# Attention, gated MLP and SoLU MLP on one core: low parts of the early weights on VectorE, low bits of twelve blocks on ScalarE, the first block's products by piece into one bank, means from split sums, and a new order

## The chip, the core and the metric

The kernel runs on one core of a Trainium2 chip. Its engines are TensorE (PE, the matmuls), VectorE (DVE), ScalarE (ACT), GpSimd (POOL) and SyncE (SP, which issues nearly all transfers). Each engine plays its own instructions in order, and semaphores hold it where an operand is missing. The metric is the time of one execution on the device in microseconds; the median of the runs shown counts.

## The reference

```python
def reference(**kwargs):
    attn_out = _attn_ref(**attn_kwargs)          # q, k, v: 4 x 8 x 576 x 64; window 32, for half the heads dilated by 4
    x = attn_out.transpose(0, 2, 1, 3).reshape(B * S, H * D)      # 2304 x 512
    x = _moe_ref(x=x, **moe_kwargs)
    return _moe2_ref(x=x, **moe2_kwargs)

def _moe_ref(x, w_gate, w_val, w_out, rms_g):    # 512 -> 1536 -> 512
    rms = np.sqrt(np.mean(x * x, axis=-1, keepdims=True) + 1e-06)
    xn = x / rms * rms_g
    g = xn @ w_gate
    silu = g * (1.0 / (1.0 + np.exp(-g)))
    return silu * (xn @ w_val) @ w_out

def _moe2_ref(x, w_in, w_out, g_ln):             # 512 -> 1024 -> 512
    h = x @ w_in
    solu = h * softmax(h)
    return layer_norm(solu) * g_ln @ w_out
```

The weights come in 64-bit words, and each is taken apart into a high and a low float32r part.

## The kernel before

Nine pieces of 256 tokens (`PIECES`, t = 0 to 8) form five parts (`PARTS`); the first part is the pieces 0 and 1. For each piece attention makes x, `rms` norms it and splits it into `xh` and `xl`, and `mlp` multiplies it with twelve blocks f of the 1536 hidden columns, each block with a gate product `g`, a value product `vp`, tanh, silu and product on ACT and DVE, and an out product into the banks y0 to y3. Every product is three in float32r, high by high, low by high and high by low (`mm3`, L952 to L954). `g` and `vp` have one PSUM bank each.

Weights: a block of 512 KB is fetched by SP (`fetch`, `raw`), shifted on ACT (`shifted`, L386), its low bits are taken on DVE (`parts`, L391), both are joined on DVE (`joined`, L395), ACT casts the high part (`halves`, L333) and DVE or POOL subtracts it for the low part (`lows`, L342). A block f has three such weights, 0 `w_gate`, 1 `w_val`, 2 `w_out`. A raw block lies where its weights will be, in slot f.

Pieces 0 and 1 are done first, as four pairs of head groups (`pair(t, m)`). Their q, k and v lie in the rooms of slots 11 to 8 (`EARLY`: pair (0,0) in 11, (0,1) in 10, (1,0) in 9, (1,1) in 8), so the weights of these slots can be fetched only when a pair's values are done. A pair runs scores (L509, L511), maximum, a centring product (L522), exponential, sum, weights, transposes (L544) and values (`pv`, L566). The later pieces go through `attention`. `rms` takes the mean of squares, for t of 2 and more as one float32 product of ones with the sum (`ms`, L827).

`mlp` runs over virtual passes: v = 0 is piece 0 with f = 0 alone, v = 1 piece 1 with f = 0 alone, both 256 columns wide, and v = 2 both pieces with the other blocks, 512 wide.

The order is made by `Plan`: each step has its needs, its buffers, a cost for each engine it may use and a due time; a greedy pass over the engines gives the order, and `play` writes the program in it. `NUDGE` shifts due times of single steps and `ENGINE` fixes engines. Where the plan has a hole on TensorE early on, `fill` (L351) issues products of a constant `seed` (128x256, bf16) into a bank that the next step takes.

Of the kernel before, what the change touches and what calls it, by code (L numbers as in the profile page):

```python
# [20 lines left out]
P = 128  # L21
# [23 lines left out]
def groups_of(piece):  # L45
# [30 lines left out]
    else:  # L76
# [7 lines left out]
        for at, bt in ((128, b), (192, b2)):  # L84
# [12 lines left out]
HALVES = 1  # L97
# [5 lines left out]
SINGLE = 7  # L103
# [6 lines left out]
NUDGE = {('centred', (1, 1)): -15.5, ('copy', (1, 0)): 10, ('copy', (3, 1)): 11, ('copy', (4, 1)): 57,  # L110
         ('copy', (5, 0)): 32, ('copy', (7, 1)): 50, ('ecomb', 5): -17, ('eload', 9): 14, ('eps', 1): -41.9,
         ('eps', 3): 13, ('ewhole', 1, 0): -45, ('ewhole', 2, 1): 35, ('ewhole', 3, 0): 48, ('ewhole', 4, 0): 15,
         ('exps', (2, 1)): 57, ('g', 2, 8, 1): 24, ('gln',): 60, ('high', 0, 0): -27, ('high', 1, 0): 35,
         ('landed', 6): -22, ('load_qk', (1, 1)): -1.6, ('load_v', (0, 0)): 3.07, ('low', 0, 1): -43.6,
         ('low', 1, 0): 93, ('low', 1, 1): -32.8, ('masking', (2, 0)): -65, ('masking', (3, 1)): -22,
         ('masking', (4, 1)): 40, ('masking', (5, 0)): 13, ('masking', (6, 0)): -65, ('maximum', (1, 0)): -3,
         ('maximum', (1, 1)): -8.1, ('maximum', (2, 0)): -98, ('maximum', (3, 1)): -45, ('maximum', (5, 1)): 78,
         ('newton', 0, 2): 58, ('norm', (0, 1)): -0.8, ('norm', (2, 1)): 31, ('out', 2, 1, 0): -124,
         ('out', 2, 1, 1): 45.1, ('out', 2, 2, 0): 7.5, ('prod', 1, 0): 28, ('prod', 3, 0): 43, ('prod', 4, 3): 23,
         ('prod', 4, 7): 71, ('rmsg',): 14, ('scale', 0, 1): -35.9, ('scale', 1, 0): -11.5, ('scale', 1, 1): -38.4,  # L120
         ('scale', 1, 2): 0.08, ('scale', 1, 4): 1, ('scale', 2, 0): -5.5, ('scale', 2, 1): -25, ('scale', 2, 3): 49,
         ('scale', 3, 0): -11.4, ('scale', 3, 1): -38.8, ('scale', 3, 4): 43, ('silu', 3, 3): 17, ('silu', 3, 4): 46,
         ('square', 0, 0): 77, ('square', 0, 1): -34.9, ('square', 1, 1): -32.9, ('square', 1, 4): -10,
         ('square', 2, 1): -42.3, ('square', 3, 1): -29.9, ('sums', (1, 0)): -45, ('sums', (1, 1)): 44,
         ('tanh', 'c11', 0): 138, ('total', 2, 0): -12, ('total', 3, 0): -9.1, ('turned0', (0, 1)): -34,
         ('turned1', (0, 1)): -38, ('uhigh', 3, 4): -68, ('ulow', 4, 2): 88, ('ulow', 4, 4): 1, ('xcomb', 't3'): 35,
         ('xcomb', 't4'): 44, ('xlow', 't1', 1): 8, ((1, 0), 'lows', 0): 19, ((1, 0), 'lows', 1): 11,
         ((1, 0), 'shifted', 2): 33, ((1, 1), 'fetch', 0): 41, ((1, 1), 'fetch', 1): 12, ((1, 1), 'fetch', 2): 6,
         ((1, 1), 'joined', 0): 5.2, ((1, 1), 'joined', 2): -10, ((1, 1), 'lows', 2): -16.5,
         ((1, 1), 'parts', 1): 10, ((1, 1), 'parts', 2): 47.5, ((1, 1), 'shifted', 1): 91,  # L130
         ((1, 1), 'shifted', 2): 41, ((1, 10), 'fetch', 2): -33, ((1, 10), 'parts', 0): 23,
         ((1, 11), 'fetch', 0): -52, ((1, 11), 'fetch', 1): 31.9, ((1, 11), 'fetch', 2): -32,
         ((1, 11), 'lows', 0): 19.5, ((1, 11), 'parts', 0): 22.9, ((1, 2), 'fetch', 1): -5,
         ((1, 2), 'joined', 1): 32, ((1, 2), 'lows', 1): 91, ((1, 2), 'parts', 0): 4.7, ((1, 2), 'parts', 1): -4,
         ((1, 2), 'parts', 2): 39, ((1, 3), 'fetch', 1): 32, ((1, 3), 'halves', 2): 8.4, ((1, 3), 'joined', 2): 18.2,
         ((1, 3), 'parts', 0): 28, ((1, 3), 'parts', 1): 11.7, ((1, 3), 'parts', 2): 35, ((1, 3), 'shifted', 0): 13,
         ((1, 4), 'fetch', 0): 45, ((1, 4), 'fetch', 1): 27, ((1, 4), 'fetch', 2): 35.82, ((1, 4), 'halves', 2): -41,
         ((1, 4), 'joined', 0): 15.8, ((1, 4), 'joined', 2): 18, ((1, 4), 'lows', 1): -4.6, ((1, 4), 'lows', 2): -20,
         ((1, 4), 'parts', 1): 3.3, ((1, 4), 'parts', 2): -25, ((1, 5), 'fetch', 0): 16, ((1, 5), 'fetch', 1): 33,
         ((1, 5), 'lows', 2): 36.9, ((1, 5), 'parts', 0): 24.1, ((1, 5), 'parts', 1): 33.9,  # L140
         ((1, 5), 'parts', 2): 11.7, ((1, 6), 'fetch', 0): -3.5, ((1, 6), 'fetch', 1): 29,
         ((1, 6), 'halves', 0): -12, ((1, 6), 'joined', 0): 28, ((1, 6), 'lows', 1): 42, ((1, 6), 'parts', 0): 24.5,
         ((1, 6), 'parts', 2): 28, ((1, 7), 'fetch', 0): 74, ((1, 7), 'fetch', 2): -54, ((1, 7), 'joined', 0): 21.7,
         ((1, 7), 'parts', 0): -29.1, ((1, 8), 'fetch', 0): -21, ((1, 8), 'fetch', 1): 82.9,
         ((1, 8), 'parts', 0): 17.8, ((1, 9), 'fetch', 1): 18.2, ((1, 9), 'parts', 0): 19}
# [43 lines left out]
class Plan:  # L189
# [20 lines left out]
    def order(self):  # L210
# [32 lines left out]
        while ready:  # L243
# [13 lines left out]
            if e == "p" and free["d"] > start:  # L257
                free["d"] += 0.45 * cost
# [27 lines left out]
def tile_attention_glu_solu(ctx: ExitStack, tc: tile.TileContext, qk_d, v_d, w1_d, win2_d, wout2_d,  # L286
# [71 lines left out]
    def prepare(stage, f, cuts, srcs, scales, dues, needs=(), lead=((1, 0), "joined", 0)):  # L358
# [65 lines left out]
        for i in range(m):  # L424
            plan.add((key, "fetch", i), {"s": 1.35}, fetch(i), needs, due=dues[i] - 12)
        for n, c in enumerate(cuts):
            w, due = 512 * len(c), dues[c[0]]
            one, two, act, pool_ = 0.15 + w / 1920, 0.15 + w / 960, 0.2 + w / 1200, 0.25 + w / 500
            plan.add((key, "shifted", n), {"a": act}, shifted(c), [(key, "fetch", i) for i in c], due=due)
            plan.add((key, "parts", n), {"d": one}, parts(c), [(key, "fetch", i) for i in c], due=due)  # L430
# [32 lines left out]
    def pair(t, m, due):  # L463
# [61 lines left out]
        def exps(e):  # L525
            nc.scalar.activation(T[s_], T[sp], AF.Exp, scale=0.125)
# [53 lines left out]
        plan.add(step("load_qk"), {"s": 2.15}, load_qk, due=due - 8)  # L580
# [1376 lines left out]
```

## Time and profile before

| what | us |
|---|---|
| runs | 711.44, 711.47, 712.87 (median 711.47) |
| the profiled execution | 712.27, span 710.2 |
| TensorE busy | 702.3 (99%), 4533 matmuls |
| DVE busy | 509.4 (72%) |
| ACT busy | 358.9 (51%) |
| POOL busy | 135.5 (19%) |
| last product's end | 707.05 |

The page gives each engine's busy time over the whole span; where TensorE waits is read from its timeline, in which a line shows in brackets how long the engine stood idle before an instruction and what ended that. An instruction's own duration runs past the start of the next on TensorE, so the time that a product takes is read from one start to the next.

### The profile page before, as it was taken

The numbers are of one execution on the slowest core, as the hardware profiler recorded it, in microseconds if no ns is written. First come the engines' busy times: TensorE is split into PE (matmuls) and PEld (weight loads), VectorE is DVE, ScalarE is ACT, GpSimd is POOL, SyncE is SP. The second block draws the span as 40 slices with busy tenths as digits, with TensorE's granted clock in tenths as the row PEclk, the third lists the DMA queues.
The fourth block names the chain that finished last, engine by engine and source line by source line (L and its number), as shares of the span: only waits on it lengthen the run. The fifth ranks groups of instructions, "written<-read, shape, count | busy, mean of one in ns | idle before, by whom it ended". The sixth has DMA issues, their size and how long they took to land.

```text
span 710.2 us, 11738 instructions
## 1 busy us (share of the span) xinstructions
PE 702.3 (99%) x4533; PEld 593.3 (84%) x4533; DVE 509.4 (72%) x932; ACT 358.9 (51%) x769; POOL 135.5 (19%) x166
## 2 busy tenths in 40 slices
PE   8999999999999999999999999999999999999998
PEld 6788888899998888888888888888888888888887
DVE  5899899679585986668966766689677677665552
ACT  2976854344535554516655554355375555543440
POOL 0322432250506121110000000014044311010110
PEclk9999999999999999999999999999999999999999
DMA  9999433154368764403321112947032111000001
GB/s 336 401 407 354 133 101 118 64 185 141 134 225 293 276 206 141 141 7 125 123 72 37 52 60 97 344 139 220 1 119 75 60 60 45 30 16 30 30 30 45
DMA packets 42424, 97.21 MB, mean 137 GB/s; under 512 B 3841, under 2 KB 14081, under 8 KB 42369
## 3 DMA queue, kind: packets, MB, share of 16 engines
q1 hardware_dynamic: 40640, 93.33, 37.9%
q10 hardware_dynamic: 1728, 3.15, 1.2%
q8 instruction: 35, 0.57, 0.3%
q14 instruction: 21, 0.16, 0.1%
HBM read 72.87 MB, written 23.59 MB: 136 GB/s over the span
## 4 chain that ended last, share of the span: by engine, by line
PE 93%; DMA 5%; ACT 1%; DVE 1%; SPq 0%; issue 0%; ACTq 0%
PE y L952 7%; PE ca L1292 7%; PE y L954 7%; PE y L953 7%; PE o L1689 5%; PE o L1688 5%; PE o L1687 5%; PE g L952 4%; PE vp L952 4%; PE g L953 4%; PE g L954 4%; PE vp L954 4%; PE vp L953 4%; DMA raw<-w 3%; PE cd L1292 2%; PE cb L1292 2%
## 5 line engine op out<-in xcount | busy, mean ns | idle before, releaser
L342 POOL TENSOR_TENSOR w<-wf,w 128x512 fp32r<-128x512 f32 (+1 forms) x15 | 25.1, 1673 | 203.9 <-ACT w L333 203.9
L1687 PE MATMUL o<-w,lt 128*128 128x512 f32 (+1 forms) x152 | 58.9, 388 | 0.0
L1689 PE MATMUL o<-w,lt 128*128 128x512 f32 (+1 forms) x152 | 57.6, 379 | 0.0
L1688 PE MATMUL o<-w,lt 128*128 128x512 f32 (+1 forms) x152 | 57.5, 379 | 0.0
L952 PE MATMUL y<-uh,w 128*128 128x512 f32 (+1 forms) x148 | 53.2, 359 | 0.0
L954 PE MATMUL y<-uh,w 128*128 128x512 f32 (+1 forms) x148 | 51.7, 349 | 0.0
L953 PE MATMUL y<-uh,w 128*128 128x512 f32 (+1 forms) x148 | 51.7, 349 | 0.0
L660 ACT ACTIVATE s<-s,nm 128x64 f32<-128x64 f32 x120 | 40.1, 337 | 18.6 <-DVE nm L655 18.6
L333 ACT CAST w<-wf 128x512 fp32r<-128x512 f32 (+1 forms) x40 | 28.3, 728 | 25.5 <-DVE wf L395 11.5
L952 PE MATMUL g<-xh,w 128*128 128x512 f32 (+1 forms) x104 | 40.4, 389 | 0.0
L333 ACT CAST uh<-u 128x512 fp32r<-128x512 f32 (+1 forms) x37 | 19.9, 537 | 38.3 <-DVE u L996 37.7
L953 PE MATMUL g<-xl,w 128*128 128x512 f32 (+1 forms) x104 | 39.0, 375 | 0.2 <-DVE xl L342 0.2
L952 PE MATMUL vp<-xh,w 128*128 128x512 f32 (+1 forms) x100 | 39.0, 390 | 0.0
L954 PE MATMUL g<-xh,w 128*128 128x512 f32 (+1 forms) x104 | 38.9, 374 | 0.0
L954 PE MATMUL vp<-xh,w 128*128 128x512 f32 (+1 forms) x100 | 38.2, 382 | 0.0
L953 PE MATMUL vp<-xl,w 128*128 128x512 f32 (+1 forms) x100 | 38.1, 381 | 0.0
L805 POOL TENSOR_TENSOR sq<-x 128x256 f32<-128x256 f32 x28 | 17.8, 647 | 105.7 <-DVE x L337 61.6
L1655 POOL TENSOR_SCALAR st<-st 128x1 f32<-128x1 f32 x18 | 8.7, 484 | 140.5 <-ACT sq L1646 140.3
L992 DVE SCALAR_TENSOR_TENSOR u<-u,g 128x512 f32<-128x512 f32 (+1 forms) x37 | 21.5, 582 | 18.3 <-ACT u L986 18.3
L986 ACT ACTIVATE u<-g 128x512 f32<-128x512 f32 (+1 forms) x37 | 19.0, 514 | 27.9 <-PE g L954 27.2
L1689 PEld LDWEIGHTS o<-w,lt 128*128 128x128 f32 x152 | 28.6, 188 | 5.3
L342 DVE TENSOR_TENSOR lt<-tp,lt 128x512 fp32r<-128x512 f32 x36 | 23.2, 684 | 13.6 <-ACT lt L333 13.6
(290 smaller groups left out, 2056.5 us busy)
## 6 DMA issues: line engine op xcount, KB each, us to landing
raw<-w SPq DMA_DIRECT2D x36, 512.0 KB, 9.1
es<-ec SPq DMA_DIRECT2D x12, 512.0 KB, 3.1
sc<-es SPq DMA_DIRECT2D x12, 512.0 KB, 3.4
qk<-qk SPq DMA_DIRECT2D x7, 800.0 KB, 5.5
vt<-v SPq DMA_DIRECT2D x10, 512.0 KB, 5.6
wo<-w SPq DMA_DIRECT2D x9, 512.0 KB, 7.6
wst<-wo SPq DMA_DIRECT2D x9, 512.0 KB, 3.7
yT<-yo SPq DMA_DIRECT2D x16, 256.0 KB, 3.1
```

The lines of the kernel that those rows point to most:

```text
L333: nc.scalar.copy(dst, src) if scale is None else nc.scalar.mul(dst, src, scale)
L342: ENG[e].tensor_tensor(dst, a, b, ALU.subtract)
L660: nc.scalar.activation(T[s_][:, i], T[s_][:, i], AF.Exp, bias=st["nm"][:, i:i + 1], accum_out=sm[:, i:i + 1])
L952: nc.tensor.matmul(acc, wh, xh, start=first, stop=False)
L953: nc.tensor.matmul(acc, wh, xl, start=False, stop=False)
L954: nc.tensor.matmul(acc, wl, xh, start=False, stop=last)
L986: return lambda e: nc.scalar.activation(new(up, ("u", v, f), [P, 512])[:, 0:n], T["g", v, f], AF.Tanh, scale=0.5)
L992: return lambda e: nc.vector.scalar_tensor_tensor(out=u_of(f), in0=u_of(f), scalar=1.0, in1=T["g", v, f], op0=ALU.add, op1=ALU.mult)
L1292: nc.tensor.matmul(acc(x), w, y, start=not more and j == 0 and n == 0, stop=j == 1 and n == 2, skip_group_check=True)
L1687: nc.tensor.matmul(o, lt[:, 0, k], w[:, 0], start=(k == 0), stop=False)
L1688: nc.tensor.matmul(o, lt[:, 0, k], w[:, 1], start=False, stop=False)
L1689: nc.tensor.matmul(o, lt[:, 1, k], w[:, 0], start=False, stop=(k == NF2 - 1))
```

## The change

It does the following.
- `cuts(f)`: the three weights of a block are handled apart for f of 0 and 1, as gate with value and out for 2 to 6, together from 7 on (before: apart up to 6). `lows` of f below 8 are for DVE alone (before: those of `w_gate` and `w_val` of f = 0 alone).
- `parts` may run on ACT (L472 of the new file), as a product with 2^-29 and a bias; twelve blocks do.
- A pair's q and k come in two transfers and its scores in two steps, with the mask as a third. Pair (0,0) (`BY_SET`) does no centring product; ACT takes eight exponentials of 64 columns with the maximum as bias and the sum as second output.
- For t of 2 and more the mean comes from the sum's high and low float32r parts (`sumhigh`, `sumlow`) by two products.
- v = 0 and v = 1 are gone: v = 2 begins with f = 0, whose `g` and `vp` are made piece by piece (`by_piece`) into the two halves of one `g` and one `vp` bank; its tanh, silu, product and out product are 512 wide.
- `fill` may issue into a bank of `by_piece` and, for the second piece, three quarters of the rest are kept.
- Costs, `PACE`, `NUDGE` and `ENGINE` have new numbers, a step `written` marks the end of a stored copy, and some buffers of the later phases change places.

```diff
+def cuts(f):
+    return [(0,), (1,), (2,)] if f < APART else [(0, 1), (2,)] if f < WIDE else [(0, 1, 2)]
...
-VIRTUAL = [(0, 0, 256, range(HALVES)), (0, 256, 256, range(HALVES)), (0, 0, 512, range(HALVES, NF1)),
-           (1, 0, 256, range(NF1)), (2, 0, 512, range(NF1))]
+VIRTUAL = {2: (0, 0, 512, range(NF1)), 3: (1, 0, 256, range(NF1)), 4: (2, 0, 512, range(NF1))}
...
+                if e == "a":
+                    nc.scalar.activation(x, x, AF.Identity, scale=2.0 ** -29 * (1 - 2.0 ** -16), bias=down)
+                else:
+                    nc.vector.tensor_scalar(x, x, 29, None, ALU.logical_shift_right)
...
-            plan.add((key, "parts", n), {"d": one}, parts(c), [(key, "fetch", i) for i in c], due=due)
+            plan.add((key, "parts", n), {"d": one, "a": act}, parts(c), [(key, "fetch", i) for i in c], due=due)
...
-            plan.add((key, "lows", n), {"d": two} if f == 0 and n < 2 else {"p": pool_, "d": two}, lows(c), [(key, "halves", n)], uses=[wf, st, (st, 1)], due=due)
+            plan.add((key, "lows", n), {"d": two} if f < LOWS_AT else {"p": pool_, "d": two}, lows(c), [(key, "halves", n)], uses=[wf, st, (st, 1)], due=due)
...
+            for i in range(8):
+                nc.scalar.activation(T[s_][:, i], T[sp][:, i], AF.Exp, scale=0.125, bias=st["nm"][:, i:i + 1], accum_out=sm[:, i:i + 1])
...
-            nc.tensor.matmul(x, ones, T["sq", t, ks[0]], start=True, stop=True)
+            for h in range(2):
+                nc.tensor.matmul(x, ones_r, T["sqh" if h == 0 else "sql", t], start=h == 0, stop=h == 1)
...
-                    if v == 1:
-                        filling[0] = 3 * filling[0] // 4
-                        fill(psy.tile([P, 512], F32, tag="y00", name="warm")[:, 0:TP])
...
+                    fill(T[key][:, 0:TP])
+                else:
+                    filling[0] = 3 * filling[0] // 4
+                    if v == 2 and filling[0] > 0:
+                        fill(psy.tile([P, 512], F32, tag="y00", name="warm")[:, 0:TP])
...
-                    alone = v == 4 and f == 0 and part == 0
+                    alone = f == 0 and (v == 2 or v == 4 and part == 0)
```

The new order at three places. On SP, the fetches behind the first weights; a `raw_0` is the first weight of its slot's room (or the whole room), `raw_1` and `raw_2` the second and third. Before, up to the gate weights of f = 1 (`raw_0_493`):

```order
L371 DMA raw_0_368<-w 128x1024 [waits DMAHW6_49]
L1839 DMA rmsg<-rmsg 128x4 [waits DMAHW7_49]
L371 DMA raw_2_384<-w 128x1024 [waits DMAHW0_49]
L371 DMA raw_1_410<-w 128x1024 [waits DMAHW1_49]
L371 DMA raw_2_441<-w 128x1024 [waits DMAHW2_49]
L371 DMA raw_0_454<-w 128x1024 [waits DMAHW3_49]
L371 DMA raw_2_471<-w 128x1024 [waits DMAHW4_49]
L371 DMA raw_0_485<-w 128x1024 [waits DMAHW5_49,PE_49]
L371 DMA raw_0_493<-w 128x1024 [waits DMAHW6_49]
```

After, up to the same weights, which are now `raw_0_512`; the fetch that waits for TensorE (`raw_0_367`) is that of slot 10:

```order
L1953 DMA rmsg<-rmsg 128x4 [waits DMAHW7_49]
L573 DMA qkv<-v 128x2x512 [waits DMAHW0_49]
L449 DMA raw_0_367<-w 128x1024 [waits DMAHW4_49,DMAHW1_49,PE_49]
L449 DMA raw_1_383<-w 128x1024 [waits DMAHW2_49]
L449 DMA raw_0_396<-w 128x1024 [waits DMAHW3_49]
L449 DMA raw_0_430<-w 128x1024
L449 DMA raw_2_441<-w 128x1024 [waits DMAHW5_49]
L449 DMA raw_2_470<-w 128x1024 [waits DMAHW6_49]
L449 DMA raw_2_480<-w 128x1024 [waits DMAHW7_49]
L449 DMA raw_0_496<-w 128x1024 [waits DMAHW0_49]
L449 DMA raw_0_504<-w 128x1024 [waits DMAHW1_49]
L449 DMA raw_0_512<-w 128x1024 [waits DMAHW2_49]
```

The wait for TensorE stood one place ahead of these gate weights; now it stands nine places ahead of them, right behind the last v.

On DVE, from the second x to the low part of the gate weights of f = 1 (`w_0_617` before, `w_0_602` after). Before, with `u<-u,g` the silu of the second piece of f = 0:

```order
L391 TENSOR_SCALAR raw_0_493<-raw_0_493 128x512 [waits DMAHW6_49]
L395 SCALAR_TENSOR_TENSOR wf<-raw_0_493 128x512 [waits DVE_49]
L342 TENSOR_TENSOR uh<-u,uh 128x256 [waits Activation_49]
L992 SCALAR_TENSOR_TENSOR u<-u,g 128x256 [waits Activation_49]
L342 TENSOR_TENSOR w_0_617<-wf,w_0_617 128x512 [waits Activation_49]
L395 SCALAR_TENSOR_TENSOR wf<-raw_1_410 128x512
L996 SCALAR_TENSOR_TENSOR u<-u,vp 128x256 [waits DVE_49,PE_49]
```

After, with `u<-u,g` the silu of both pieces:

```order
L420 TENSOR_TENSOR xl<-x,xh 128x2x256 [waits Activation_49] x2
L478 SCALAR_TENSOR_TENSOR wf<-raw_2_480 128x512
L478 SCALAR_TENSOR_TENSOR wf<-raw_0_512 128x512 [waits DMAHW2_49,Activation_49]
L478 SCALAR_TENSOR_TENSOR wf<-raw_2_470 128x512 [waits DMAHW6_49]
L478 SCALAR_TENSOR_TENSOR wf<-raw_1_383 128x512
L420 TENSOR_TENSOR w_0_602<-wf,w_0_602 128x512 [waits Activation_49]
L1100 SCALAR_TENSOR_TENSOR u<-u,g 128x512 [waits Activation_49]
L1104 SCALAR_TENSOR_TENSOR u<-u,vp 128x512 [waits DVE_49,PE_49]
L420 TENSOR_TENSOR w_2_626<-wf,w_2_626 128x512 [waits Activation_49]
L420 TENSOR_TENSOR w_1_623<-wf,w_1_623 128x512
L420 TENSOR_TENSOR uh<-u,uh 128x512 [waits Activation_49]
```

The silu of f = 0 stood ahead of these low parts and now stands behind them and behind three joins.

On ACT, around the same weights (`raw_0_493`, then `raw_0_512`). Before:

```order
L986 ACTIVATE u<-g 128x256 [waits PE_49]
L386 ACTIVATE raw_0_493<-raw_0_493 128x512 [waits DMAHW6_49]
L333 CAST xh<-x 128x2x256 [waits DVE_49] x2
L386 ACTIVATE raw_0_521<-raw_0_521 128x512 [waits DMAHW7_49]
L386 ACTIVATE raw_1_410<-raw_1_410 128x512 [waits DMAHW1_49]
L333 CAST uh<-u 128x256 [waits DVE_49]
L986 ACTIVATE u<-g 128x256 [waits PE_49]
L333 CAST w_0_617<-wf 128x512 [waits DVE_49,Activation_49]
```

After:

```order
L464 ACTIVATE raw_2_480<-raw_2_480 128x512 [waits DMAHW7_49]
L411 CAST xh<-x 128x2x256 [waits DVE_49] x2
L472 ACTIVATE raw_0_512<-raw_0_512,down 128x512 [waits DMAHW2_49]
L464 ACTIVATE raw_0_512<-raw_0_512 128x512
L411 CAST w_2_599<-wf 128x512 [waits DVE_49,Activation_49]
L411 CAST w_0_602<-wf 128x512 [waits DVE_49]
L1094 ACTIVATE u<-g 128x512 [waits PE_49]
L411 CAST w_1_623<-wf 128x512 [waits DVE_49]
```

The shift of these weights stood ahead of the casts `xh<-x` of the second piece; now their low bits and their shift stand behind those casts and ahead of the tanh of f = 0.

## Rows read from the trace of the kernel before

**Rows 1.** Page: busy us, share and instructions by engine; shares of the chain that ended last.

```profile
PE 702.3 (99%) x4533; PEld 593.3 (84%) x4533; DVE 509.4 (72%) x932; ACT 358.9 (51%) x769; POOL 135.5 (19%) x166
...
PE 93%; DMA 5%; ACT 1%; DVE 1%; SPq 0%; issue 0%; ACTq 0%
```

**Rows 2.** Timeline, TensorE: start us, us, line, operation, tiles, idle before <-what ended it.

```profile
197.10 0.63 PE L675 MATMUL tp<-ident,s 128*128 128x128 f32 x4 [0.53 <-DVE s L668]
```

**Rows 3.** Stretches: us, busy (x) of PE, PEld, DVE, ACT, POOL, PEclk, DMA share, GB/s.

```profile
15.40:16.67 1.27, 0.02 (x1) 0.03 (x1) 1.27 (x3) 0.57 (x1) 0.00 (x0) 1.00 1.01 384
36.00:41.00 5.00, 4.81 (x41) 4.60 (x39) 4.89 (x11) 3.92 (x8) 0.00 (x0) 1.00 1.02 413
40.96:200.00 159.04, 158.51 (x1281) 139.99 (x1280) 132.51 (x223) 86.06 (x227) 51.65 (x49) 1.00 0.49 176
200.00:707.05 507.05, 507.05 (x2812) 423.48 (x2810) 347.55 (x647) 247.11 (x496) 77.60 (x102) 1.00 0.32 106
```

**Rows 4.** Timeline of TensorE in the first 41 us.

```profile
16.67 1.15 PE L566 MATMUL pv<-xp,qkv 128*64 128x64 f32 x32 [1.25 <-DMA qkv<-v]
17.76 1.12 PE L522 MATMUL sp<-nm,ident 128*128 128x512 f32 x2
18.72 0.27 PE L351 MATMUL warm<-seed 128*128 128x256 bf16 x1
...
35.17 1.18 PE L351 MATMUL warm<-seed 128*128 128x256 bf16 x9
36.11 0.36 PE L952 MATMUL g<-xh,w 128*128 128x256 f32 x1
...
39.52 0.28 PE L952 MATMUL y<-uh,w 128*128 128x256 f32 x1
...
40.96 0.40 PE L952 MATMUL g<-xh,w 128*128 128x512 f32 x1
```

**Rows 5.** Chain of waits up to 37 us: start us, us, what.

```profile
3.77 11.42 DMA qkv<-v
...
25.67 9.00 DMA raw<-w
...
34.69 0.68 ACT raw L386
```

**Rows 6.** Timeline of TensorE around one mean.

```profile
107.42 0.39 PE L954 MATMUL y<-uh,w 128*128 128x512 f32 x1
107.65 0.59 PE L827 MATMUL ms<-sq,ones 128*128 128x256 f32 x2
...
108.31 0.39 PE L953 MATMUL g<-xl,w 128*128 128x512 f32 x1
```

**Rows 7.** Timeline of ACT from 36 us.

```profile
36.31 1.25 ACT L386 ACTIVATE raw<-raw 128x512 f32<-128x512 f32 x2
...
38.69 0.62 ACT L333 CAST w<-wf 128x512 fp32r<-128x512 f32 x1
```

**Rows 8.** Timeline of DVE from 39 us.

```profile
39.35 0.69 DVE L342 TENSOR_TENSOR w<-wf,w 128x512 fp32r<-128x512 f32 x1
...
44.00 0.69 DVE L395 SCALAR_TENSOR_TENSOR wf<-raw 128x512 uint32<-128x512 uint32 x1
44.61 0.68 DVE L992 SCALAR_TENSOR_TENSOR u<-u,g 128x512 f32<-128x512 f32 x1
...
46.00 1.66 DVE L395 SCALAR_TENSOR_TENSOR wf<-raw 128x512 uint32<-128x512 uint32 x1
```

**Rows 9.** Timeline of POOL at 45.7 us.

```profile
45.72 1.38 POOL L342 TENSOR_TENSOR w<-wf,w 128x512 fp32r<-128x512 f32 x1 [2.99 <-ACT w L333]
```

**Rows 10.** Page, DMA issues: tiles, queue, count, KB each, median us to landing.

```profile
sc<-es SPq DMA_DIRECT2D x12, 512.0 KB, 3.4
...
wst<-wo SPq DMA_DIRECT2D x9, 512.0 KB, 3.7
```

**Rows 11.** Page, group of instructions: line, engine, tiles, count, busy us, mean ns, idle before.

```profile
L660 ACT ACTIVATE s<-s,nm 128x64 f32<-128x64 f32 x120 | 40.1, 337 | 18.6 <-DVE nm L655 18.6
```

More of the change, by code (lines that the diff above doesn't have):

```diff
@@ L95 @@
 EARLY = {(t, m): NF1 - 1 - 2 * t - m for t in range(2) for m in range(2)}
-HALVES = 1
+BY_SET = ((0, 0),)
 X_ELSEWHERE = 4
 X_AT = 7
-SINGLE = 7
+APART, WIDE = 2, 7
+LOWS_AT = 8
+def cuts(f):
+    return [(0,), (1,), (2,)] if f < APART else [(0, 1), (2,)] if f < WIDE else [(0, 1, 2)]
 SLACK = {"t": 0.02, "a": 0.1, "d": 0.15, "p": 0.25, "s": 0.05}
 DUE_GROUP, DUE_NEXT, DUE_NORM, DUE_WEIGHTS, DUE_SLOT, DUE_THIRD = (0, 3.4), 1.66, (3.2, 13.3), 9.1, 3.0, 57.6
[L110 to L145, printed above, removed]
@@ L257, in order @@
             if e == "p" and free["d"] > start:
-                free["d"] += 0.45 * cost
+                free["d"] += (0.45 if any(str(x).endswith(("low", "lows")) for x in name) else 0.12) * cost
             done[name] = (e, start + cost)
@@ L491, in load_v, with scores, emit, masked @@
                               in_=v_d[at_:at_ + 2].rearrange("g p w -> p g w"))
-        def scores(e):
-            x = new_bank(sp, [P, 8, 64], "sp")
-            fill(x.rearrange("p s k -> p (s k)"))
+        def scores(y):
+            def emit(e):
+                x = T[sp] if y else new_bank(sp, [P, 8, 64], "sp")
+                if y == 0:
+                    fill(x.rearrange("p s k -> p (s k)"))
+                for i in range(4):
+                    for c in range(2):
+                        b = 4 * (i // 2) + 2 * c + i % 2
+                        k0 = 512 + g["offs"][b]
+                        nc.tensor.matmul(x[64 * c:64 * c + 64, 4 * y + i, :], qk()[:, y, 64 * b:64 * b + 64],
+                                         qk()[:, y, k0:k0 + 64], start=y == 0 and i == 0, stop=False)
+            return emit
+        def masked(e):
+            x = T[sp]
             n = g["mask"]
@@ L586, in pair @@
-        plan.add(step("exps"), {"a": 0.65}, exps, [step("centred")], uses=[sp, s_], due=due)
-        plan.add(step("sums"), {"d": 0.69}, sums, [step("exps")], uses=[s_], due=due)
-        plan.add(step("norm"), {"d": 0.38}, norm, [step("sums")], due=due)
+        plan.add(step("load_qk"), {"s": 1.08}, load_qk(0), due=due - 8)
+        plan.add(step("load_qk2"), {"s": 1.08}, load_qk(1), due=due - 8, after=[step("load_qk")])
+        plan.add(step("load_v"), {"s": 1.35 if t else 1.65}, load_v, due=due - 6)
@@ L589, in pair @@
+        plan.add(step("norm"), {"d": 0.38}, norm, [step("exps" if K in BY_SET else "sums")], due=due)
         plan.add(step("weights"), {"d": 0.7}, weights, [step("norm")], uses=[s_], due=due)
-        plan.add(step("transposes"), {"t": 0.66}, transposes, [step("weights")], takes=[(banks[1], tp)], uses=[s_], due=due)
+        plan.add(step("transposes"), {"t": 0.5}, transposes, [step("weights")], takes=[(banks[1], tp)], uses=[s_], due=due)
         for r in range(2):
```

238 lines of the change are left out of this document (169 added, 69 removed), and 22 rows, old and new, of tables (ENGINE, NUDGE).

## The prediction

> **What bounds the kernel now.** I read the page first: TensorE is busy for 99% of the span, and 93% of the chain that ended last is TensorE [rows 1]. So an edit counts if it takes time from TensorE or makes it wait. The waits of TensorE come next: all but one of the long ones lie before 37 us, the longest 1.25 us for the first v [rows 4], the late one 0.5 us [rows 2]. The busy time by stretch says the same [rows 3]: from 40.96 to 200 TensorE is idle for 0.53 us, and from there to 707.05 not at all, with the clock granted at 1.00. In the timeline [rows 4] the first block's value product (`vp`, second piece) ends at 39.52, the first block's out product takes 39.52 to 40.96 and covers what is still missing for the second block, and g(f=1), the second block's gate product, starts at 40.96. Up to there transfers set the time: the chain runs through `raw<-w` landings into ACT and DVE [rows 5], and the queue moves 413 GB/s at a share of 1.02 [rows 3], so a 512 KB block (524,288 bytes) passes in 1.27 us.
>
> So there are two questions: where TensorE stands when it leaves the first block's `vp`, and how much it still has to do after that. Before, that second part is 39.52 to 707.05, 667.53 us, with one wait of 0.53 in it.
>
> **Means from split sums.** Seven means, one for each piece from the third on, become two float32r products each. Before, 107.65 to 108.31 holds one mean (two rows) and one 512-wide product [rows 6]; such a product takes 0.23 (107.42 to 107.65), so a mean costs 0.43. The new two are 256 wide at 0.12 each (39.52 to 40.96 is 12 of them [rows 4]), 0.24. Gain: 7 x 0.19 = 1.33 us, all on the path. The extra cast on ACT (about 0.4) and subtraction on DVE or POOL sit in the norm of a piece that is used much later. TensorE did not wait for any L827 successor before, so I cost them at nothing; without that cover they are about 1 us for each mean.
>
> **The first block 512 wide.** Its out product was 24 products of 256 columns, 24 x 0.12 = 2.88; now 12 of 512, 12 x 0.227 = 2.72. Gain 0.16.
>
> **Lows by DVE, low bits by ACT.** Twelve 512-wide subtractions leave POOL, where one takes 1.38 [rows 9], and cost 0.69 on DVE [rows 8]. Beside that one a join on DVE (46.00) took 1.66 instead of 0.69 [rows 8], so DVE loses about as much beside POOL as it now does itself. Twelve low-bit steps (0.42 on DVE) go to ACT at about 0.6. Both engines have idle time after 41 us while TensorE has none, so I cost this at nothing there; before 41 us it is in the next sum.
>
> **Start: where the second block's gate weights come.** The DMA order changes most. Before, `w_gate` of f=1 landed at 25.67 + 9.00 = 34.67 [rows 5]. After, SP has four v and two blocks issued and then stands at the fetch into slot 10, whose room holds pair (0,1); it waits for that pair's values, and the gate weights of f=1 are the tenth block from there. Step by step:
> - Pair (0,0)'s v: before, the first v landed at 3.77 + 11.42 = 15.19 [rows 5]. One weight block now stands ahead of it: 16.46.
> - Values of (0,0) take 1.09 (16.67 to 17.76), then comes the centring product, 0.96 (17.76 to 18.72), then the values of (0,1), 1.09 [rows 4]. From 16.46 this is 19.6 at the least. The second values also need their weights from ACT, so I take 20.0, with bounds 19.6 and 20.3.
> - The pipe has run dry by then. Issue to landing of 512 KB without much of a queue ahead is 3.4 to 3.7 (sc, wst) [rows 10], and 9.00 with a full one [rows 5]; I take 3.7, as wst is a read of weights like this one, and 5.0 as the far bound, since little is left in flight by then. First block 23.7; tenth 9 x 1.27 later, 35.1.
> - ACT does low bits and the shift of that block together, 1.25 as two such shifts took [rows 7]: 36.35. DVE joins it, 0.65 [rows 8]: 37.05 with the handing over. ACT casts it, 0.62 [rows 7]: 37.67, then does the tanh of f=0, as wide a step: 38.25.
> - DVE, in order, joins two more blocks (0.61 each, 38.3), makes the lows (0.65, 38.95) and only then does silu of f=0 (0.61): 39.6 (rows that last 0.69 follow one another after 0.61, as 44.00 is followed at 44.61 [rows 8]). Silu reads the g bank, of which there is one.
> - Nine warm-up products into the g bank cannot start before that: 0.94 for nine [rows 4]. g(f=1) starts at 40.55.
>
> The x of the second piece lies ahead of that block on ACT, not behind it as before, where xh had to wait for the shift at 34.69 [rows 5]; so `vp` ends 0.7 to 1.5 us earlier, at about 38.0 to 38.8. That gains nothing, since the bank is late: TensorE waits 0.8 to 1.6 us and then fills. Against 39.52, when the same amount of work remained, the start loses **1.03 us**. Bounds: the same data as before lies ahead of that block in the queue, so it can't land before 34.67; with that and a bank 0.3 earlier the loss is 0.3. SP at 20.3 and 5.0 give +2.6.
>
> The Trainium skill ("DMA: Bandwidth & Descriptors", Anatomy of one DMA) gives a fixed 2.0 us and the bytes at 436 GB/s, there for the other way of issuing: 3.2 us instead of my 3.7. By it g(f=1) would start 0.5 us earlier; the rows show nothing below 3.4 for a read of this size, so they decide.
>
> **The start of attention.** The scores are split by set, and pair (0,0) takes eight exponentials with sums on ACT instead of a centring product, one exponential and a sum on DVE. All that stands before v lands, for which TensorE waited 1.25 us [rows 4]; cost nothing. If the cover is gone it is eight steps of 0.34 on ACT [rows 11] against 0.96 on TensorE and two steps of about 0.65, some 0.4 us.
>
> **The one wait later.** At 197.10 TensorE waited 0.53 for DVE's weights of a pair [rows 2]. The distance in TensorE's work from that pair's scores to its transposes is about the same in the new order, so its end is not assured. I take half, 0.27, with bounds 0 and 0.53.
>
> **Sum.** +1.03 - 1.33 - 0.16 - 0.27 = -0.73 us. The profiled execution took 712.27 (span 710.2 and 2.1 around it), so 711.5; it was 0.8 above the median of 711.47. On the median the forecast is **710.7 us**. A measurement of this kernel can tell about 0.2%, 1.42 us, from no change; this is within it.
>
> **Rivals.**
> 1. *The bank is no limit.* If SP gets going before the pipe is dry, the ten blocks follow the last v without a hole, and the tenth lands at 34.7, as the gate weights did before [rows 5]; with 0.2 less on DVE ahead of silu, g(f=1) starts near 39.9 and the later wait goes too: +0.4 - 1.49 - 0.53 = -1.6, 709.9; with 0.4 less again -2.0, 709.5. For it: the queue ran full in the whole start before (1.01 at 15.40 to 16.67, 1.02 later [rows 3]). Against: slot 10's wait hangs on a chain that ends at 19.6 at the earliest. Chance 0.32.
> 2. *The stand is longer* (slower). Place: SP at slot 10; all that g(f=1) needs stands behind it in one line (block, ACT, DVE's silu, bank, fills), so every us there is a us at the end. It decides at a loss of 2.9 us, when the tenth block lands after 37.0. A landing of 5.0 with the time of two blocks (2.5) lost in the refilled queue would do it: +3.8 - 1.49 = +2.3, 713.8. Against: the queue moved 413 GB/s whenever it had work. Chance 0.11.
> 3. *It does not do what it says*: the means' new casts delay the norms, and TensorE waits out the 0.19 it saves. Then +1.03 - 0.16 = +0.9 at the most, 712.3; it stays within 0.2%. Chance 0.07, inside "same".
> 4. *The clock falls in the new wait.* It stayed at 1.00 through 15.40 to 16.67, where TensorE did almost nothing [rows 3], and the wait that I expect is no more than 0.4 us longer. If it fell to the lower of its two levels, 1.2 GHz, a 512-wide product would take 0.45 for 0.23, and the twelve of g(f=1) 2.7 us more: 713.4. Chance 0.02. The Trainium skill ("TensorE: Matmul & The Clock Gate", Part 1) says that an idle TensorE is throttled and that activity releases it; the trace has no stretch that shows the lower level.
>
> **Numbers.** Forecast (with rival 3) 0.55, rival 1 0.32, rivals 2 and 4 together 0.13. Faster by over 0.2% 0.32, within 0.2% 0.55, slower by over 0.2% 0.13. The range runs from rival 1's far bound, 709.5, to the forecast's upper bound with part of rival 2, 712.9.
>
> **What will show it.** In the timeline of TensorE: `vp` of the second piece ends near 38.4, then a wait of about a microsecond named after DVE's silu, nine fills, g(f=1) near 40.5. On SP a gap before the fetch at about 20.0 and the tenth landing near 35.1. Means with two rows of about 0.12 each. From g(f=1) to the last product about 666.0. Wrong would be: a start before 40.0 or after 42, a wait of over 0.5 us after it, or a clock below 1.00 behind the wait.

## The result, and the profile after

The changed kernel takes 718.1 us (median of four runs, 717.84 to 718.87), the kernel before 711.83 beside it on the same chip: a ratio of 1.0088 [1.0070, 1.0105]. It is slower by 6.3 us, where the forecast was 0.8 faster and the range ended at 712.9. The profiled execution took 718.87, its span is 717.1.

Page of the changed kernel, as [rows 1]: busy us, share and instructions by engine; then the chain that ended last.

```profile
PE 708.3 (99%) x4536; PEld 594.0 (83%) x4536; DVE 512.4 (71%) x961; ACT 382.9 (53%) x815; POOL 63.0 (9%) x91
...
PE 94%; DMA 4%; SPq 1%; DVE 1%; ACT 0%; issue 0%
```

TensorE is busy for 6.0 us more than before with 3 matmuls more. So part of the loss is no wait at all: the same work got longer. The stretches answer to [rows 3] (columns as there; the eighth figure, PEclk, is the granted clock):

```profile
17.80:24.00 6.20, 6.13 (x92) 4.92 (x91) 5.46 (x13) 4.31 (x9) 0.00 (x0) 1.00 0.68 236
24.00:25.00 1.00, 0.83 (x4) 0.83 (x5) 1.00 (x4) 0.00 (x0) 0.71 (x1) 0.61 1.02 418
25.00:26.00 1.00, 1.00 (x9) 0.50 (x8) 0.36 (x2) 0.73 (x2) 0.00 (x0) 0.50 0.98 270
26.00:27.00 1.00, 1.00 (x22) 1.00 (x22) 0.74 (x1) 1.00 (x4) 0.00 (x0) 0.50 1.01 365
27.00:28.00 1.00, 1.00 (x17) 0.89 (x14) 0.18 (x1) 1.00 (x3) 0.00 (x0) 0.69 0.92 303
28.00:43.87 15.87, 13.59 (x131) 12.04 (x130) 14.36 (x29) 11.32 (x20) 1.87 (x2) 1.00 1.02 406
43.87:200.00 156.13, 156.13 (x1258) 137.42 (x1256) 130.35 (x220) 98.19 (x237) 23.55 (x26) 1.00 0.49 175
200.00:713.39 513.39, 513.39 (x2835) 425.75 (x2834) 352.74 (x681) 258.30 (x521) 36.20 (x52) 1.00 0.32 107
```

From 43.87, where g(f=1) starts, to the last product at 713.39 TensorE never waits and its clock is 1.00; the late wait of 0.53 [rows 2] is gone. Still this stretch takes 669.52, where about 666 was expected. The timeline of TensorE, as [rows 4], has the rest of the loss in its last two lines:

```profile
17.80 1.15 PE L661 MATMUL pv<-xp,qkv 128*64 128x64 f32 x32
18.88 1.13 PE L610 MATMUL sp<-nm,ident 128*128 128x512 f32 x2
19.94 1.15 PE L661 MATMUL pv<-xp,qkv 128*64 128x64 f32 x32
...
40.84 0.28 PE L1065 MATMUL vp<-xh,w 128*128 128x256 f32 x1
42.95 1.17 PE L429 MATMUL g<-seed 128*128 128x256 bf16 x9 [1.83 <-DVE u L1100]
43.87 0.48 PE L1063 MATMUL g<-xh,w 128*128 128x512 f32 x1
```

The form is the one forecast: `vp` ends, TensorE waits for DVE's silu, nine fills, g(f=1). But g(f=1) starts at 43.87 and not at 40.55; before, the same amount of work remained at 39.52 [rows 4]. The chain of waits, as [rows 5], tells how it came to that (start us, us, what):

```profile
5.52 9.57 DMA qkv<-qk
...
15.23 0.69 PE sp L585 x16
...
16.85 0.59 PE tp L639 x4
...
17.87 1.08 PE pv L661 x32
18.95 1.05 PE sp L610 x2
20.01 1.11 PE pv L661 x32
21.11 0.02 issue
21.13 0.33 SPq L449
...
21.50 4.51 DMA raw<-w
...
26.03 12.37 DMA raw<-w
...
38.43 0.78 ACT raw L472
...
39.80 1.90 DVE wf L478 x3
41.70 0.60 DVE w L420
42.30 0.61 DVE u L1100
```

Read it from above: a q-k transfer, scores, transposes, the values of pair (0,0), the centring product, the values of (0,1); only then SP issues the fetch into slot 10 (`SPq L449` at 21.13). The tenth block from there lands at 38.41 (26.03 + 12.37), then come ACT, three joins, a low part, silu. The waits of SP from 14 to 45 us (engine, line, what it waited for, us, times, longest) put the stand at 2.7 us:

```profile
SPq L449 <- PE pv L661: 2.7, 1, 2.7
```

So three things are to be explained: the start (43.87 against 39.52, +4.35), the stretch behind it (669.52 against 667.53 before from 39.52 on, although means and a wait were saved there), and the end: from the last product to the end of the span it is 3.10 before and 3.70 after, +0.6.

### The profile page after: what moved, and what is told of

The parts are those of the page before. It is cut to its first block, busy times and chain, and to the rows that moved or that the text cites. A ratio compares the mean times of both kernels' runs of the same rounds, so it can differ in the third digit from the quotient of the medians.

```text
span 717.1 us, 11699 instructions
## 1 busy us (share of the span) xinstructions
PE 708.3 (99%) x4536; PEld 594.0 (83%) x4536; DVE 512.4 (71%) x961; ACT 382.9 (53%) x815; POOL 63.0 (9%) x91
## 4 chain that ended last, share of the span: by engine, by line
PE 94%; DMA 4%; SPq 1%; DVE 1%; ACT 0%; issue 0%
PE y L1063 7%; PE ca L1406 7%; PE y L1065 7%; PE y L1064 7%; PE o L1803 5%; PE o L1801 5%; PE o L1802 5%; PE vp L1063 4%; PE g L1063 4%; PE g L1065 4%; PE vp L1065 4%; PE g L1064 4%; PE vp L1064 4%; DMA raw<-w 2%; PE cc L1406 2%; PE cb L1406 2%
## 5 line engine op out<-in xcount | busy, mean ns | idle before, releaser
L1063 PE MATMUL y<-uh,w 128*128 128x512 f32 (+1 forms) x144 | 51.7, 359 | 0.0
L1065 PE MATMUL y<-uh,w 128*128 128x512 f32 (+1 forms) x144 | 51.0, 354 | 0.0
L1064 PE MATMUL y<-uh,w 128*128 128x512 f32 (+1 forms) x144 | 50.9, 354 | 0.0
L411 ACT CAST w<-wf 128x512 fp32r<-128x512 f32 (+2 forms) x35 | 27.5, 806 | 14.3 <-PE y L1065 6.1
L1803 PEld LDWEIGHTS o<-w,lt 128*128 128x128 f32 x152 | 28.6, 188 | 5.5
L1802 PEld LDWEIGHTS o<-w,lt 128*128 128x128 f32 x152 | 28.7, 189 | 5.0
L1801 PEld LDWEIGHTS o<-w,lt 128*128 128x128 f32 x152 | 28.6, 188 | 4.9
L1104 DVE SCALAR_TENSOR_TENSOR u<-u,vp 128x512 f32<-128x512 f32 (+1 forms) x36 | 21.5, 596 | 14.7 <-PE vp L1065 14.0
L420 DVE TENSOR_TENSOR w<-wf,w 128x512 fp32r<-128x512 f32 (+2 forms) x32 | 29.4, 929 | 3.1 <-ACT w L411 3.1
```

Of the source, the lines that this page charges most:

```text
L411: nc.scalar.copy(dst, src) if scale is None else nc.scalar.mul(dst, src, scale)
L420: ENG[e].tensor_tensor(dst, a, b, ALU.subtract)
L1063: nc.tensor.matmul(acc, wh, xh, start=first, stop=False)
L1064: nc.tensor.matmul(acc, wh, xl, start=False, stop=False)
L1065: nc.tensor.matmul(acc, wl, xh, start=False, stop=last)
L1104: return lambda e: nc.vector.scalar_tensor_tensor(out=u_of(f), in0=u_of(f), scalar=0.5, in1=T["vp", v, f], op0=ALU.mult, op1=ALU.mult)
```

## The experiments

All kernels but the fourth and the ninth compute everything. "Behind" is the time from the start of g(f=1) to the last product, the largest stretch in which nothing waits; it and "g(f=1)" come from each kernel's profiled execution (us). The ratio is that to the kernel before in the same set of runs.

| kernel | median | ratio, interval | g(f=1) | behind |
|---|---|---|---|---|
| before | 711.83 | | 40.96 | 666.09 |
| after | 718.1 | 1.0088 [1.0070, 1.0105] | 43.87 | 669.52 |
| e1 after, 32 bytes more | 716.67 | 1.0078 [1.0061, 1.0095] | 42.05 | 668.35 |
| e2 before, 32 bytes more | 715.26 | 1.0049 [1.0034, 1.0064] | 39.95 | 669.54 |
| e3 after, slot 10 fetched later | 716.15 | 1.0065 [1.0050, 1.0080] | 41.07 | 669.55 |
| e5 after, 224 bytes more | 714.32 | 1.0035 [1.0023, 1.0048] | 43.18 | 665.14 |
| e6 e5 and e3 together | 711.53 | 0.9996 [0.9987, 1.0006] | 41.62 | 665.13 |
| e7 e6 without nine fills | 711.27 | 0.9994 [0.9985, 1.0003] | 40.04 | 665.39 |
| e8 e7, silu earlier | 711.58 | 0.9996 [0.9986, 1.0005] | 39.71 | 665.62 |
| e10 e5 with the whole mean | 715.70 | 1.0057 [1.0043, 1.0071] | 42.51 | 666.73 |

(g(f=1) of before stands behind the first block's out product; the start that compares with the others is 39.52.)

**Longer products.** In the middle of the program both kernels do the same products, with TensorE never idle. The stretches of 20 us at 380 and 540, before and then after:

```profile
380.00:400.00 20.00, 20.00 (x90) 16.56 (x89) 13.18 (x19) 10.93 (x18) 0.00 (x0) 1.00 0.18 53
540.00:560.00 20.00, 20.00 (x98) 16.73 (x97) 14.00 (x33) 12.28 (x21) 10.89 (x15) 1.00 0.13 41
```

```profile
380.00:400.00 20.00, 20.00 (x89) 16.31 (x88) 13.23 (x19) 11.11 (x19) 0.00 (x0) 1.00 0.19 64
540.00:560.00 20.00, 20.00 (x92) 16.40 (x91) 17.00 (x43) 12.56 (x22) 2.64 (x5) 1.00 0.24 73
```

Fewer products pass in the same time at the same clock (98 and 92 partly because the stretches hold other steps). Product by product, from one start to the next, a 512-wide float32r product takes 0.2267 or about 0.233, and which of them goes with its tiles: those of a weight in a lower tile with an operand in an upper one, or the other way round, take 0.233. The built program says where in SBUF each tile lies, and what the change did to that is small. It added two constants, `ones_r` of 512 bytes and `down` of 4 (which take 32), and so every tile that is placed from the lower side of SBUF (weights, xh, xl) moved from 224 to 0 modulo 256 bytes, while those placed from the upper side stayed at 224. The first two experiments move the lower tiles by 32 bytes, in the kernel after and in the kernel before:

```diff
+    spare = const.tile([P, 1], F32, name="spare")
...
+    nc.gpsimd.memset(spare, 0.0)
```

> The changed kernel with one more constant of 32 bytes behind `down`, which moves every tile of the lower part of SBUF from an address of 0 mod 64 to one of 32 mod 64, where they lay before the change; nothing else differs. Theory A (a product is slower when its two operands lie differently within 64 bytes): the 512-wide products of `ca<-xt,shl` and `ha<-w,yh` go from 0.233 back to 0.227, the work behind g(f=1) from 669.5 to about 665.5, the time from 718.1 to about 714. Theory B (the longer products come from what the other engines do meanwhile, which is the same here): 718, within 0.3 us.

> The kernel before with one more constant of 32 bytes, so that its lower tiles lie at 0 mod 64 and the upper ones stay at 32 mod 64, as in the changed kernel. Theory A: its products with mixed operands go from 0.227 to 0.233, some 3 to 4 us more, 715 to 716. Theory B: 711.8, no change.

Measured: e2 is slower than the kernel before by 0.49%, and all of it lies behind g(f=1): 669.54 for 666.09, +3.45, with a start that was even 1.0 earlier. Its stretch at 380 holds 89 products for 90, like that of the changed kernel:

```profile
380.00:400.00 20.00, 20.00 (x89) 16.30 (x88) 12.87 (x19) 10.93 (x18) 0.00 (x0) 1.00 0.16 52
```

One unused constant of 4 bytes did that, so the place of the tiles costs time, whatever else the change does. e1 brought back 1.2 of it only; equality modulo 64, by which both were expected to go, does not decide. The next kernel measures products alone (no attention, no MLP), moving and stationary operands at four places each:

```diff
+    for rnd in range(3):
+        for o in range(4):
+            for q in range(4):
+                for k in range(24):
+                    c = 128 * (k % 4)
+                    nc.tensor.matmul(acc[n // 12 % 4], ws[q][:, c:c + 128], xs[o], start=n % 12 == 0, stop=n % 12 == 11)
+                    n += 1
```

> Products alone: three rounds of 16 groups of 24 float32r products, 512 wide, with moving and stationary operand at 0, 16, 32 or 48 bytes past a multiple of 64; no other engine works and the result is no attention. Theory A: groups whose operands lie alike within 64 bytes take 0.227 for a product, the others about 0.233. Theory B: all groups take the same.

Measured: the pairs lie between 0.2267 and 0.2343, and each repeats to 0.0002 in the second and third round; but the equal offsets are not those at 0.2267. The tiles of this kernel start at other places modulo 256, so that no pair was equal in that. It shows that the time is a matter of two addresses, and that modulo 64 is not the rule; what it shows against modulo 256 stands behind e9. e5 makes the lower tiles equal to the upper ones modulo 256 again:

```diff
+    spare = const.tile([P, 56], F32, name="spare")
```

> The changed kernel with a constant of 224 bytes behind `down`, so that all operands of the 512-wide products lie at 224 mod 256, as they all did before; with 32 bytes the lower tiles lay at 32 and the upper ones at 224 mod 256. Theory A (the two operands must lie alike modulo 256): the work from g(f=1) to the last product goes from 669.5 to about 665.5, against 668.4 with 32 bytes; the time to about 714, with the start as late as it was, or 712 if the clock does not fall either. Theory B (what helped was 32 mod 64 alone): about 668.4 again, and 716.7.

Measured: 665.14 for 669.52 behind g(f=1), 4.38 us back, and the two stretches are as before's again:

```profile
380.00:400.00 20.00, 20.00 (x90) 16.57 (x89) 12.63 (x18) 11.55 (x19) 0.00 (x0) 1.00 0.16 53
540.00:560.00 20.00, 20.00 (x98) 16.75 (x97) 17.47 (x42) 12.40 (x22) 4.73 (x8) 1.00 0.13 42
```

The last of these runs products alone once more, with all tiles starting at the same place modulo 512 and offsets in steps of 32 bytes:

> Products alone, no attention and no MLP: 512-wide float32r products whose moving and stationary operands lie at 8 x 8 offsets of 0, 32, ... 224 bytes behind multiples of 256, 24 products for each pair, in two rounds. If the time goes by the distance between the two addresses modulo 256, the table is constant along its diagonals, fast on the main one (0.2267) and slow (0.233) off it. If it goes by one operand's own place, whole rows or whole columns are slow. If it goes by neither (each tile has its own further address bits), the slow places show no pattern, and the rule stays at what the kernel's own runs show: all operands at one place modulo 256 is fast.

Measured, us of one product from start to start, by the offset of the moving operand (rows) and of the stationary one (columns), second round; the first round is the same to 0.0002 but for its first groups:

```
        0      32     64     96     128    160    192    224
  0   .2279  .2334  .2334  .2343  .2336  .2333  .2289  .2332
 32   .2335  .2279  .2334  .2335  .2343  .2336  .2333  .2289
 64   .2289  .2334  .2267  .2334  .2335  .2343  .2335  .2333
 96   .2334  .2290  .2332  .2267  .2334  .2335  .2343  .2335
128   .2336  .2333  .2289  .2332  .2267  .2335  .2335  .2343
160   .2340  .2324  .2333  .2289  .2333  .2267  .2334  .2335
192   .2333  .2343  .2335  .2333  .2290  .2332  .2267  .2335
224   .2329  .2335  .2343  .2336  .2333  .2289  .2332  .2267
```

The table is nearly constant along its diagonals: the time goes by the distance, modulo 256, from the stationary operand's address to the moving one's (moving at 64 with stationary at 0 is like 0 with 192). It is fast at 0 (0.2267, but for two entries at 0.2279), a third of the way to slow at 64 (0.2289), and slow elsewhere (0.2324 to 0.2343).

This is shown for addresses on multiples of 32, as the tiles of the kernels before and after have them, and not beyond. In e4 the four pairs with both operands on such addresses agree with the table (0.233 to 0.234 at distances of 160, 192 and 224). Pairs with both operands 16 bytes past a multiple of 32 do not: moving at 16 and stationary at 112 modulo 256 (distance 160) took 0.2267, and so did 48 and 80 (distance 224). What decides there stays open.

With the table the kernels' own products can be read, by the same distance:

| kernel | lower with lower | lower moving, upper weights | upper moving, lower weights |
|---|---|---|---|
| before | 0: 0.2267 to 0.2272 | 0: 0.2267 to 0.2272 | 0: 0.2267 to 0.2272 |
| after | 0: 0.2281 | 32: 0.2330 (326 products) | 224: 0.2338 (72 products) |
| e1 | 0: 0.2280 | 64: 0.2302 | 192: 0.2333 |

e1's partial gain is the entry at 64. In the kernel after, the 398 products with mixed tiles cost 2.4 us. The other 2.0 lie at products whose own operands match: 82 of them are followed by one whose weights lie off, and these take 0.2348, 0.6 us together. The weight load of the next product runs beside the product (PEld overlaps PE), so it may be that the two reads meet; that is not shown. Some 1.3 us are spread over 1,811 matching products (19% of them over 0.2295, 7% before). About 0.3 of that lies at 94 that come right behind a mixed one (0.2303 in the mean); the rest stays unexplained.

**The start.** e3 takes the stand of SP away from the gate weights: the fetch into slot 10 is issued behind theirs.

```diff
+        late = steps.pop(names.index(((1, 10), "fetch", 0)))
+        steps.insert([x[2] for x in steps].index(((1, 1), "fetch", 0)) + 1, late)
```

> The changed kernel with the fetch into slot 10, at which SP stood until 21.1 us, put behind the fetch of the second block's gate weights. Theory A (the stand and the pipe that runs dry make the gate weights late): they land at 34 to 35 instead of 38.4, and g(f=1) starts at 41 to 42 instead of 43.9, then bound by the second piece's value product, which ended at 40.96; 2 to 3 us less, 715 to 716. Theory B (the weights would come late anyway, by slow packets and by instruction fetches in the queue): under 1 us less.

Measured: the gate weights land at 33.51 for 38.41, g(f=1) starts at 41.07 for 43.87, and the wait shrinks from 1.83 to 0.6 (waits of TensorE, 14 to 45 us):

```profile
PE g L429 <- DVE u L1100: 0.6, 1, 0.6
```

So the stand was 2.8 us of the 4.35 in these two executions; the ratios put the later fetch at 1.6 us (1.0088 and 1.0065) and, for e5 and e6 of one set, at 2.8. Behind it the next line is DVE, whose two `xl`, four joins and a low part run without a hole into silu (its timeline):

```profile
34.98 1.46 DVE L420 TENSOR_TENSOR xl<-x,xh 128x512 fp32r<-128x512 f32 x2
36.36 2.54 DVE L478 SCALAR_TENSOR_TENSOR wf<-raw 128x512 uint32<-128x512 uint32 x4
38.81 0.68 DVE L420 TENSOR_TENSOR w<-wf,w 128x512 fp32r<-128x512 f32 x1
39.41 0.68 DVE L1100 SCALAR_TENSOR_TENSOR u<-u,g 128x512 f32<-128x512 f32 x1
```

e6 joins this to e5; e7 sets the nine fills to none, and e8 puts silu ahead of two of the joins, with the gate weights joined and cast first:

```diff
+                if name == ("g", 2, 1, 0):
+                    filling[0] = 0
...
+        chain = [("silu", 2, 0), ((1, 1), "joined", 1), ((1, 1), "halves", 1), ((1, 1), "joined", 2), ((1, 1), "halves", 2)]
+        for behind, name in zip(chain, chain[1:]):
+            move(name, behind)
```

> The changed kernel with the constant of 224 bytes and with the fetch into slot 10 behind that of the second block's gate weights. Theory A (alignment and the stand are two separate costs): g(f=1) at 41.1 as with the later fetch alone, 665.5 behind it, 712 or a little less. Theory B (they overlap): more than 713.

> The one before, and without the nine warm-up products into the g bank. Theory A (they stand in the line to g(f=1)): 0.9 us less than e6_pad_fetch. Theory B (the clock falls without them): 1 to 3 us more, with a granted clock below 1.00 behind 40 us.

> The one before, and on DVE the joins of the second block's value and out weights behind the silu of the first block instead of ahead of it, the gate weights joined and cast first. Theory A (silu waits behind joins that nothing needs yet): g(f=1) up to 1.2 us earlier than in e7_no_fill, 710 or less. Theory B (the joins that are put off delay the value product of the second block as much): no change.

Measured: with both repairs (e6) the changed kernel is level with the one before, 0.9996. Without the fills (e7) g(f=1) starts 1.6 earlier (40.04 for 41.62), 0.6 of it because `vp` ended earlier in that execution, and TensorE still waits 0.6 for silu. The medians differ by 0.3 only, so neither theory holds as stated: A had 0.9 less, B 1 to 3 more. e8 starts 0.33 earlier than e7 and takes 0.23 longer behind; the 710 of its theory A was not reached. Over ten runs each none of the three can be told from the kernel before, so the change has no version here that beats it.

**The means.** e10 makes the mean whole again in the kernel of e5; the cast and the subtraction for the split sum are still made, with no reader.

```diff
-            for h in range(2):
-                nc.tensor.matmul(x, ones_r, T["sqh" if h == 0 else "sql", t], start=h == 0, stop=h == 1)
+            nc.tensor.matmul(x, ones, whole, start=True, stop=True)
```

> The changed kernel with the padding of 224 bytes, and the mean of t of 2 and more made again as one float32 product of ones with the sum; the cast and the subtraction for the split sum are still made, and nobody reads their results. The order of all else is that of the padded kernel. If the means' term of the forecast holds (7 x 0.19), the stretch from g(f=1) to the last product is 1.3 longer than the 665.14 of the padded kernel, 666.5, and the time is 1.3 above it. If the new order gained what the sum put down to the means, it stays at 665.1.

Measured: 666.73 for 665.14 behind g(f=1), 1.59 us for seven means. The timeline around one of them, first e10, then the changed kernel:

```profile
109.20 0.60 PE L776 MATMUL tp<-ident,s 128*128 128x128 f32 x4
109.63 0.60 PE L929 MATMUL ms<-sq,ones 128*128 128x256 f32 x2
109.88 0.58 PE L1064 MATMUL vp<-xh,w 128*128 128x512 f32 x1
110.30 0.40 PE L1065 MATMUL vp<-xl,w 128*128 128x512 f32 x1
```

```profile
110.56 0.60 PE L775 MATMUL tp<-ident,s 128*128 128x128 f32 x4
110.92 0.37 PE L928 MATMUL ms<-sqh,ones_r 128*128 128x256 f32 x1
111.12 0.28 PE L928 MATMUL ms<-sql,ones_r 128*128 128x256 f32 x1
111.24 0.39 PE L1063 MATMUL vp<-xh,w 128*128 128x512 f32 x1
111.46 0.40 PE L1064 MATMUL vp<-xl,w 128*128 128x512 f32 x1
```

From the transposes to the second product behind the mean it is 1.10 and 0.90: 0.20 for one mean, as forecast (0.19).

## Why the prediction was wrong

Where the 6.9 us of span (717.1 against 710.2) come from:

| term | forecast | measured | from |
|---|---|---|---|
| start | +1.03 | +4.35 | 43.87 against 39.52 |
| place of the operands | none | +4.38 | after against e5 |
| means | -1.33 | -1.59 | e10 against e5 |
| first block's out product | -0.16 | -0.15 | 24 products at 0.12 before, 12 at 0.227 after; not tried alone |
| late wait | -0.27 | -0.53 | [rows 2]; none after |
| end, behind the last product | 0 | +0.6 | 3.70 against 3.10 |
| left over | | -0.1 | |

**The step that failed first** is one that the sum does not have: "from g(f=1) to the last product about 666.0" takes each product at its price in the trace of before, and the two new constants are costed at nothing since no engine waits for them. They shift the tiles, and with the tiles the price of the 398 mixed products and of others beside them, by 4.38 us in all. e2 shows it with nothing else changed, e5 takes it back. With this alone repaired (e5) the median is 714.3, still above the range, so the start failed by itself as well. Nothing in the rows of before warned of it, since there all tiles lay alike; but the new constants stand in the diff, and the addresses of the built program could have been compared. By the Trainium skill ("SBUF — State Buffer", "SBUF: two separate sides") TensorE never waits for another reader of SBUF, as only the port pair that DVE and GpSimd share brings contention. The price here, 0.2267 or about 0.233, went by the distance of TensorE's own two operands, with other engines at work (e2) and without (e9); so the measurement decides.

**The start** had the right mechanism and the wrong sizes; it is rival 2, to which the prediction gave 0.11. Its point of decision was a tenth block behind 37.0 and a loss of 2.9 us; the block landed at 38.41, and the loss was 4.35. (That rival's own example leaves out the 1.03 that the start loses already: with it 3.8 becomes 4.8, and its time 714.8 and not 713.8.) By the forecast's steps:
- SP released at 20.0: it was 21.13, +1.1. From the first values on the steps were right (17.87 to 21.11 is 3.24, the sum had 3.14 from 16.46 to its lower bound of 19.6). But the forecast let pair (0,0) begin with the landing of its v, 16.46. That came from a landing at 15.19 which was pair (0,1)'s; the v of pair (0,0), for which TensorE waited until 16.67 [rows 4], landed at 16.54. After, it landed at 17.16, and its values stood longer than that, behind the scores of pair (1,1), whose q and k landed from 15.09 on, and the transposes of pair (0,1): TensorE ran these, two masks and two fills from 15.23 to 17.80 without a wait. "All that stands before v lands" was the wrong cover.
- First block 3.7 after the issue: 3.59 (24.72). By the Trainium skill ("DMA: Bandwidth & Descriptors", Anatomy of one DMA), whose fixed part and rate are given for the other way of issuing, the estimate was 3.2; the trace does not agree.
- Nine more blocks at 1.27, 11.4: they took 13.7, +2.3. Seven came at 1.22 to 1.30, but one took 2.45 and another 2.49. In the stretches from 25 to 28 us the queue's share is 0.92 to 1.01 while the rate falls to 270, 365 and 303 GB/s. Beside the late one, at 31.9, a fetch of 16 KB of instructions stands in the trace; but the kernel before has such a fetch at 30.2 beside steps of 1.26 to 1.29, so it is not shown to be the cause. The early one has no such neighbour, and several packets of 4 KB took 0.5 to 1.1 us. A long step early on, at 27.6 to 28.5, is in e1 (2.74) and e10 (2.30) as well, and not in e5; in e3, where SP does not stand there, no step from 23 to 36 is over 1.30.
- Landing to g(f=1) 5.45: 5.46. ACT, three joins, the low part, silu and nine fills cost what the rows said.

How much of this is the run's luck, other executions show: the same start in e1, e5 and e10 has SP's issue at 19.97, 21.48 and 20.12, the tenth block at 36.59, 37.70 and 37.05, and g(f=1) at 42.05, 43.18 and 42.51. So even the best of four loses 2.5, near the upper bound of 2.6, and e10's block at 37.05 goes with a loss of 3.0, as the point of decision had it. The chain as it ran in e5:

```profile
21.48 0.33 SPq L450
...
21.85 4.72 DMA raw<-w
26.59 11.11 DMA raw<-w
37.72 0.78 ACT raw L473
```

A refilled queue was taken for as quick as a full one from its first block on; the rows of before, which never show it empty, could not carry that. Three of the four executions lose more than the 2.9 of rival 2, so its chance of 0.11 was too low.

**Right** were the means, the price of ACT's and DVE's new work behind g(f=1) (no wait there at all), the late wait's direction, the form of the wait at the bank, and the `vp` that ends before the bank is free; it ended late too, at 40.96 for 38.4, by the same late start. **The clock** (rival 4) stayed at 1.00 through the new wait. It fell earlier, from 24.2 to 27.6, to the lower of its two levels (0.50), behind a stretch in which TensorE was busy for 6.13 of 6.20 us with values, transposes and one-column products. The values of a pair took 1.97 there for 1.15. It is not what made the start late: from 21.13 the chain runs through SP, transfers, ACT and DVE, and e1, whose clock was 1.00 throughout, waited 1.74 for the same silu.

**Open** are the 0.6 at the end (all versions of the changed kernel have 3.68 to 3.72 behind the last product; the last store's packets and a fetch of 8 KB of instructions that begins 1.5 us behind them, 0.45 before, stand there, but it was not tried), the slow packets near 26 us, most of the 1.3 us of matching products that are slow, and addresses off the multiples of 32.

## What to carry to other kernels

A new constant is not free because nobody waits for it: it moves the tiles behind it, and where a product's two operands, both on multiples of 32 bytes, then differ in their address modulo 256, a 512-wide float32r product costs about 0.233 for 0.2267 (0.2289 at 64); pad so that they agree, and compare the stretch with the most products before and after a change. A wait on a transfer queue can cost more than its own length (here 2.7 us of waiting and, against e3, a landing 4.9 us later, of which 1.25 is the block that e3 puts behind): count the first landing anew, take more than the full queue's step for the blocks behind it, and place the wait behind the transfers that are due first.

## What the runs showed of the hardware

- The time of a 512-wide float32r product goes by the distance from its stationary to its moving operand in SBUF, modulo 256 bytes, where both lie on multiples of 32: 0.2267 at 0, 0.2289 at 64, 0.2324 to 0.2343 at the other multiples of 32 (e9), in two rounds alike. With both 16 bytes past such a multiple it does not (e4).
- From 25 to 28 us, soon after the stand, the queue's share was 0.92 to 1.01 at 270 to 365 GB/s, where it moved 413 at 1.02 in the kernel before [rows 3].
- The granted clock fell to 0.50, the lower of its two levels, at 24.2 us, behind a stretch with TensorE busy for 6.13 of 6.20 us, and stayed at 1.00 in the wait of 1.83 us that came later.
